# A load ring regrouped from nine 16 KB slots to five 32 KB slots in a decode attention kernel

## The chip, the cores and the metric

The kernel runs on one core of a Trainium2 chip. The metric is device time in microseconds; lower is better. "Span" is the time from the first to the last instruction in a profile or a timed run; the device time was 1.8 to 3.0 us longer in the runs of the record.

## The reference

One decode token attends over a cache of 65,536 keys and values for 4 key-value heads (8 query heads each, head size 128), beside a small gated MLP; a sigmoid gate mixes the two. Cut to what matters:

```python
# x: (1,1,1024); k_cache, v_cache: (1,4,65536,128); wq: (1024,4096); wo: (4096,1024), all bfloat16
g = sigmoid((x * gate_w).sum(-1))
a = softmax(q(x @ wq) @ k.T / sqrt(128)) @ v @ wo      # 8 query heads per k/v head
b = mlp(x, w_in, w_sp, b_sp, w_out)                     # w_in: (1024,3584), w_out: (1792,1024)
out = g * a + (1 - g) * b
```

Every byte of cache and weights is needed once: 162 MB, of which keys and values are 134 MB.

## The kernel before

A recorder notes each operation with what it reads and writes and turns that into semaphore waits. All large loads go from HBM (the chip's main memory) through one ring of buffers, the slots, in SBUF (the core's own memory, 128 partitions) and one queue, issued by SyncE (SP). A *unit* is 16 KB per partition: 8,192 keys of one head, or a piece of weights.

```python
TILES = 64; UK = 128 * TILES          # keys in a unit
NS = 9; SLOT = 8192                   # nine slots of 8192 bf16 = 16 KB per partition
NKTS = 8; NSC = 12                    # buffers for transposed keys, for scores
# [...]
small(vw(xT, 0, [[2, 4], [1, 2]]), A_x[0, 0].rearrange("(i p k) -> p i k", i=4, k=2), "xT")   # 512 pieces of 4 B
small(vw(gw, 0, [[2, 4], [1, 2]]), gate_w.rearrange("(i p k) -> p i k", i=4, k=2), "gw")      # on ScalarE's queue
# [...]
def kv(cache, g, u):
    return cache[0, g, UK * u:UK * (u + 1), :].rearrange("(p x) d -> p (x d)", p=128)
# stream: 4 x wq, keys 0..7 with w_in and w_out between them, then key n and value n-9 in turn, 4 x wo
def issue(upto):
    while issued[0] < min(upto, len(stream)):
        n = issued[0]
        key, src, ln = stream[n]
        s = n % NS
        P("SP", lambda e, n=n, src=src, ln=ln: e.dma_start(slot(n)[:, 0:ln], src), w=[("slot", s)], dma="s%d" % s)
        issued[0] += 1
# [...] the last PE operation that reads a slot is followed by issue(place[key] + NS + 1)
```

A step on TensorE (PE) transposes one key unit (64 transposes), makes its scores, and multiplies the softmax weights of a unit nine steps back with its values. PE's first operation needs the gate vector `gw`; its last is the output projection on the four `wo` loads.

Of the kernel before, what the change touches and what calls it, by code (L numbers as in the profile page):

```python
# [137 lines left out]
def bass_gated_mix__gqa_block_cached__mixer_gmlp__decode_kernel(  # L138
# [25 lines left out]
    TILES = 64  # L164
    UK = 128 * TILES
    NU = Sk // UK
    NS = 9
    SLOT = 8192
    NB = TILES // 8
    NKTS = 8  # L170
    NSC = 12
    QW = DO // 4
    SCALE = 1.0 / math.sqrt(Dh)
    GELU_C = 0.044715
# [52 lines left out]
    def slot(n):  # L227
        return ab("RING", SLOT, (n % NS) * SLOT)

# [28 lines left out]
    def small(dst, src, key):  # L258
        def f(e):
            with nc.allow_non_contiguous_dma(reason="a few bytes"):  # L260
                return e.dma_start(dst, src)
        P("ACT", f, w=[key], dma=key)

    small(vw(xT, 0, [[2, 4], [1, 2]]), A_x[0, 0].rearrange("(i p k) -> p i k", i=4, k=2), "xT")
    small(vw(gw, 0, [[2, 4], [1, 2]]), gate_w.rearrange("(i p k) -> p i k", i=4, k=2), "gw")
    small(wb[:, 0:1], bass.AP(tensor=B_w_sp.tensor, offset=B_w_sp.offset, ap=[[0, 128], [1, 1]]), "wsp")
    small(wb[:, 1:2], bass.AP(tensor=B_b_sp.tensor, offset=B_b_sp.offset, ap=[[0, 128], [1, 1]]), "bsp")


    stream = []  # L270
    place = {}

    def load(key, src, n):
        place[key] = len(stream)
        stream.append((key, src, n))

    def rows(w, i, c):

        return w[128 * c * i:128 * c * (i + 1), :].rearrange("(p c) n -> p (c n)", c=c)

    WQ_N = HQ * Dh

    def kv(cache, g, u):
        return cache[0, g, UK * u:UK * (u + 1), :].rearrange("(p x) d -> p (x d)", p=128)

    KV = [(g, u) for g in range(G) for u in range(NU)]
    for i in range(4):
        load(("wq", i), rows(A_wq, i, 2), 2 * WQ_N)
    steps = []
    for n in range(NU):  # L290
        load(("k", n), kv(A_k_cache, *KV[n]), SLOT)
        aux = None
        if n < 4:
            load(("win", n), rows(B_w_in, n, 2), 2 * F)
            aux = ("win", n)
        elif n in (5, 7):
            i = (n - 5) // 2
            load(("wout", i), rows(B_w_out, i, 7), 7 * DO)
            aux = ("wout", i)
        steps.append((n, None, aux))  # L300
    total = G * NU
    for n in range(NU, total + NU + 1):
        k = n if n < total else None
        v = n - NU - 1
        if k is not None:
            load(("k", k), kv(A_k_cache, *KV[k]), SLOT)
        if v >= 0:
            load(("v", v), kv(A_v_cache, *KV[v]), SLOT)
        else:
            v = None  # L310
        steps.append((k, v, None))
    for i in range(4):
        load(("wo", i), rows(A_wo, i, 8), 8 * DO)

    issued = [0]

    def issue(upto):
        while issued[0] < min(upto, len(stream)):
            n = issued[0]
            assert n < NS or stream[n - NS][0] in used  # L320
            key, src, ln = stream[n]
            s = n % NS
            P("SP", lambda e, n=n, src=src, ln=ln: e.dma_start(slot(n)[:, 0:ln], src), w=[("slot", s)], dma="s%d" % s)
            issued[0] += 1

    used = set()

    def use(key):
        issue(place[key] + 1)
        used.add(key)  # L330
        return slot(place[key]), ("slot", place[key] % NS)

    issue(NS)

# [22 lines left out]
    for i in range(4):  # L357
        sl, key = use(("wq", i))

        def f(e, i=i, sl=sl):  # L360
            for k in range(2):
                for h in range(HQ):
                    ins = e.matmul(pf(OB)[:, h:h + 1], sl[:, WQ_N * k + 128 * h:WQ_N * k + 128 * (h + 1)],  # L363
                                   xT[:, 2 * i + k:2 * i + k + 1], start=(i == 0 and k == 0 and h == 0),
                                   stop=(i == 3 and k == 1), skip_group_check=True)
            return ins
        P("PE", f, r=["xT", key], w=[B(OB)])
        issue(place[("wq", i)] + NS + 1)
    for g in range(G):
        P("DVE", lambda e, g=g: e.tensor_copy(vw(qpad, 128 * g, [[40, 4], [1, 8]]),  # L370
                                              vw(pf(OB), 8 * g, [[0, 4], [1, 8]])),
# [6 lines left out]
    def k_piece(n, j):  # L378
        sl, key = use(("k", n))
        first = nbatch[0]  # L380
        for b in (2 * j, 2 * j + 1):
            i = nbatch[0]
            nbatch[0] += 1
            pb = KTB[i % 4]

            def tr(e, b=b, pb=pb):
                for t in range(8):
                    ins = e.transpose(pbf(pb)[:, 128 * t:128 * (t + 1)],  # L388
                                      sl[:, 128 * (8 * b + t):128 * (8 * b + t + 1)], idb)
                return ins  # L390
            P("PE", tr, r=["idb", key], w=[B(pb)])
            if b in (2, 5, 7):
                P("ACT", lambda e, i=i, pb=pb: e.activation(ktb(i), pbf(pb), ACTF.Copy),  # L393
                  w=[("kt", i % NKTS), B(pb)])
            else:
                P("DVE", lambda e, i=i, pb=pb: e.tensor_copy(ktb(i), pbf(pb)), w=[("kt", i % NKTS), B(pb)])  # L396
        if j == 3:
            issue(place[("k", n)] + NS + 1)
        pend.append((n, j, first))

    def s_piece():
# [46 lines left out]
    def pv_piece(n):  # L448
        g, u = KV[n]
        sl, key = use(("v", n))  # L450

        def f(e):
            for xi in range(4):
                for cg in range(4):
                    ins = e.matmul(pf(OB)[32 * cg:32 * (cg + 1), :],  # L455
                                   ptsb(n)[:, 128 * xi + 32 * cg:128 * xi + 32 * (cg + 1)],
                                   vw(sl, 128 * (4 * cg + xi), [[2048, 4], [1, 128]]),
                                   start=(u == 0 and xi == 0), stop=(u == NU - 1 and xi == 3),
                                   tile_position=(0, 32 * cg), skip_group_check=True)
            return ins  # L460
        P("PE", f, r=[("ptsb", n % 2), key], w=[B(OB)])
        issue(place[("v", n)] + NS + 1)
        if u == NU - 1:
            out_piece(g)

# [30 lines left out]
    def win_piece(i):  # L496
        sl, key = use(("win", i))

        def f(e):
            for k in range(2):  # L500
                for z in range(2 * FC):
                    c0 = F * k + FH * (z // FC) + 128 * 7 * (z % FC // 7) + z % 7
                    ins = e.matmul(pf(MB)[:, z:z + 1], vw(sl, c0, [[7, 128]]), xT[:, 2 * i + k:2 * i + k + 1],  # L503
                                   start=(i == 0 and k == 0 and z == 0), stop=(i == 3 and k == 1),
                                   skip_group_check=True)
            return ins
        P("PE", f, r=["xT", key], w=[B(MB)])
        issue(place[("win", i)] + NS + 1)
        if i == 3:
            mixer_piece()  # L510

# [33 lines left out]
    def wout_piece(i):  # L545
        sl, key = use(("wout", i))

        def f(e):
            for c in range(7):
                for q in range(4):  # L550
                    ins = e.matmul(pf(MB)[32 * q:32 * q + 1, 0:QW], yb[:, 7 * i + c:7 * i + c + 1],  # L551
                                   sl[:, DO * c + QW * q:DO * c + QW * (q + 1)],
                                   start=(i == 0 and c == 0), stop=(i == 1 and c == 6), tile_position=(0, 32 * q),
                                   skip_group_check=True)
            return ins
        P("PE", f, r=["yb", key], w=[B(MB)])
        issue(place[("wout", i)] + NS + 1)
        if i == 1:
            P("ACT", lambda e: e.activation(brow[0:97, :], pf(MB)[0:97, 0:QW], ACTF.Copy), w=["brow", B(MB)])

# [8 lines left out]
    for si, (k, v, aux) in enumerate(steps):  # L569
        nxt = steps[si + 1][1] if si + 1 < len(steps) else None  # L570
        if k is None and pend:
            s_piece()
        if v is not None and v not in started:
            start_exp(v)
        for j in range(4):
            if k is not None:
                k_piece(k, j)
                s_piece() if len(pend) > 1 else None
            if j == 1 and v is not None:
                pt_piece(v)  # L580
            if j == 2 and nxt is not None and (k is not None or not pend):
                start_exp(nxt)
            if j == 3 and v is not None:
                pv_piece(v)
        if v is not None and v % NU == 0:
            weight_piece(v // NU)
        if aux is not None:
            (win_piece if aux[0] == "win" else wout_piece)(aux[1])


    FB = KTB[0]
# [46 lines left out]
```

## Time and profile before

| | before |
|---|---|
| device time, median | 395.0 us (394.81 to 395.49) |
| span in the profile | 393.2 us |
| HBM bytes read | 162.01 MB |
| PE busy | 70% |
| last output weights used from | 388.76 us |

The first view is the page's head, the slices and the DMA part of the kernel before: busy time by engine, then the busy share (tenths) and the GB/s of 40 equal slices of the span, then packets and bytes by queue.

```profile
span 393.2 us, 8544 instructions
...
PE 275.8 (70%) x3902; PEld 195.3 (50%) x3902; DVE 160.4 (41%) x347; ACT 124.3 (32%) x171; POOL 1.5 (0%) x8
...
DMA  8999999999999999999999999999999999999992
GB/s 318 403 427 422 419 429 423 423 423 428 430 427 427 424 425 425 427 427 426 423 423 425 427 428 428 427 428 428 427 425 427 421 428 425 427 426 430 425 397 89
...
q1 hardware_dynamic: 11240, 162.01, 97.3%
q8 instruction: 31, 0.51, 0.5%
q10 hardware_dynamic: 1344, 0.00, 0.2%
...
HBM read 162.01 MB, written 0.00 MB: 412 GB/s over the span
```

The DMA engines hardly rest: 162.01 MB at 427 GB/s are 379 us. PE is not the limit. A packet is one entry of the DMA engines' records; here it holds one row of one partition (9,216 packets of 16 KB for 72 loads of 128 rows). Beside the data queue (q1) stand 31 packets of an instruction queue (q8), 16 KB each, and 1,344 packets (q10) of the small loads.

The chain that ended last, in order of time (start, length, what), shows where compute decides and where loading does. Five of its pieces:

```profile
1.22 38.99 DMA arena<-in_gate_w_dram
...
165.67 35.17 DMA arena<-in_A_k_cache_dram
...
346.71 41.91 DMA arena<-in_A_wo_dram
388.76 1.91 PE pb L598 x26
390.69 0.42 DVE arena L604
```

PE starts after the gate's 39 us, works off its backlog until about 166 us, and from then on waits for loads.

Two readings below come from the records of the trace that the page only sums up: each DMA packet with its start, duration and size, and each increment of a load's semaphore. The profile counts 16 DMA engines, and a load of the kernel before has 16 increments ("landings"). I take one increment as one engine's share of the load, eight of its 128 packets, and their spread as how far apart the engines are. The last load before, with the first landing in us and the offsets of the others in ns:

```
before, last wo load: first landing 381.95
offsets 0 123 135 147 611 776 899 3065 4833 4922 6318 6379 6392 6437 6449 6677
```

Seven engines are within 0.9 us of each other. Eight are 4.8 to 6.7 us behind; one lies between, at 3.1 us. The kernel can end only after the last of them, at 388.62 us. I call the first group the leading engines and the other one the lagging engines. At 47 us this spread is only 0.6 us.

### The profile page before, as it was taken

The numbers are of one execution on the slowest core, as the hardware profiler recorded it, in microseconds if no ns is written. First come the engines' busy times: TensorE is split into PE (matmuls) and PEld (weight loads), VectorE is DVE, ScalarE is ACT, GpSimd is POOL, SyncE is SP. The second block draws the span as 40 slices with busy tenths as digits, with TensorE's granted clock in tenths as the row PEclk, the third lists the DMA queues.
The fourth block names the chain that finished last, engine by engine and source line by source line (L and its number), as shares of the span: only waits on it lengthen the run. The fifth ranks groups of instructions, "written<-read, shape, count | busy, mean of one in ns | idle before, by whom it ended". The sixth has DMA issues, their size and how long they took to land.

```text
span 393.2 us, 8544 instructions
## 1 busy us (share of the span) xinstructions
PE 275.8 (70%) x3902; PEld 195.3 (50%) x3902; DVE 160.4 (41%) x347; ACT 124.3 (32%) x171; POOL 1.5 (0%) x8
## 2 busy tenths in 40 slices
PE   0000699996998999997867686779668875644543
PEld 0000688885776766665645464556445553211121
DVE  2000043446666766576534354466334454200200
ACT  1000033332556555553524242335233334210000
POOL 1000000000000000000000000000000000000000
PEclk9999999886999999998989698889888898555555
DMA  8999999999999999999999999999999999999992
GB/s 318 403 427 422 419 429 423 423 423 428 430 427 427 424 425 425 427 427 426 423 423 425 427 428 428 427 428 428 427 425 427 421 428 425 427 426 430 425 397 89
DMA packets 12620, 162.57 MB, mean 413 GB/s; under 512 B 2596, under 2 KB 2600, under 8 KB 2600
## 3 DMA queue, kind: packets, MB, share of 16 engines
q1 hardware_dynamic: 11240, 162.01, 97.3%
q8 instruction: 31, 0.51, 0.5%
q10 hardware_dynamic: 1344, 0.00, 0.2%
q14 instruction: 5, 0.04, 0.0%
HBM read 162.01 MB, written 0.00 MB: 412 GB/s over the span
## 4 chain that ended last, share of the span: by engine, by line
DMA 60%; PE 31%; DVE 6%; ACT 1%; issue 1%; ACTq 0%; DVEq 0%
DMA arena<-in_A_k_cache_dram 30%; PE pb L388 16%; DMA arena<-in_A_wo_dram 11%; DMA arena<-in_gate_w_dram 10%; DMA arena<-in_A_v_cache_dram 10%; PE pb L410 6%; DVE arena L396 3%; PE pb L503 3%; PE pb L455 2%; PE pb L363 2%; DVE arena L415 2%; PE pb L443 1%; ACT arena L393 0%; PE pb L598 0%; PE pb L551 0%
## 5 line engine op out<-in xcount | busy, mean ns | idle before, releaser
L388 PE MATMUL pb<-arena 128*128 128x128 bf16 x2048 | 154.4, 236 | 27.5 <-DMA arena<-in_A_k_cache_dram 27.5
L388 PEld LDWEIGHTS pb<-arena 128*128 128x128 bf16 x2048 | 133.1, 107 | 55.6 <-DMA arena<-in_A_k_cache_dram 33.1
L396 DVE COPY arena<-pb 128x1024 bf16<-128x1024 bf16 x160 | 108.4, 689 | 109.8 <-PE pb L388 109.0
L393 ACT ACTIVATE arena<-pb 128x1024 bf16<-128x1024 bf16 x96 | 97.9, 1020 | 161.8 <-PE pb L388 161.8
L410 PE MATMUL pb<-arena 128*32 128x512 bf16 x512 | 54.9, 419 | 5.5 <-DVE arena L415 3.6
L455 PE MATMUL pb<-arena 128*32 128x512 bf16 x512 | 40.1, 441 | 19.0 <-DMA arena<-in_A_v_cache_dram 18.3
L455 PEld LDWEIGHTS pb<-arena 128*32 128x32 bf16 x512 | 14.3, 104 | 32.8 <-issue 20.2
L348 PE MATMUL pb<-arena 128*128 128x1 f32 x2 | 0.6, 362 | 40.7 <-DVE arena L347 40.7
L436 ACT ACTIVATE arena<-arena 128x512 bf16<-128x512 f32 x32 | 22.8, 713 | 16.3 <-PE pb L443 14.5
L446 DVE COPY arena<-pb 128x512 bf16<-128x512 bf16 x32 | 13.6, 424 | 30.4 <-PE pb L443 30.4
L410 PEld LDWEIGHTS pb<-arena 128*32 128x32 bf16 x512 | 13.3, 93 | 22.0 <-DVE arena L415 6.6
L415 DVE TENSOR_SCALAR_CACHE_REDUCE arena<-pb 128x512 f32<-128x512 f32 x32 | 21.8, 681 | 2.8 <-PE pb L410 2.8
L348 PEld LDWEIGHTS pb<-arena 128*128 128x128 f32 x2 | 0.5, 310 | 40.7 <-DVE arena L347 40.7
L443 PE MATMUL pb<-arena 128*128 128x128 bf16 x128 | 15.4, 257 | 0.0
L346 DVE TENSOR_TENSOR arena<-arena 128x8 f32<-128x8 bf16 x1 | 0.2, 166 | 37.0 <-DMA arena<-in_gate_w_dram 37.0
L443 PEld LDWEIGHTS pb<-arena 128*128 128x128 bf16 x128 | 9.1, 113 | 11.7 <-issue 11.7
L598 PE MATMUL pb<-arena 128*1 128x256 bf16 x128 | 7.5, 413 | 8.8 <-DMA arena<-in_A_wo_dram 8.8
L503 PEld LDWEIGHTS pb<-arena 128*128 128x128 bf16 x224 | 12.3, 153 | 0.9 <-issue 0.9
L503 PE MATMUL pb<-arena 128*128 128x1 bf16 x224 | 12.6, 192 | 0.0
L350 ACT ACTIVATE arena<-pb 128x1 f32<-128x1 f32 x1 | 0.2, 171 | 34.2 <-PE pb L348 34.2
L598 PEld LDWEIGHTS pb<-arena 128*1 128x1 bf16 x128 | 3.7, 115 | 12.3 <-DMA arena<-in_A_wo_dram 6.7
L363 PE MATMUL pb<-arena 128*128 128x1 bf16 x256 | 7.1, 165 | 1.8 <-issue 1.8
(78 smaller groups left out, 60.5 us busy)
## 6 DMA issues: line engine op xcount, KB each, us to landing
arena<-in_A_k_cache_dram SPq DMA_DIRECT2D x32, 2048.0 KB, 29.9
arena<-in_A_v_cache_dram SPq DMA_DIRECT2D x32, 2048.0 KB, 37.5
arena<-in_A_wq_dram SPq DMA_DIRECT2D x4, 2048.0 KB, 14.8
arena<-in_A_wo_dram SPq DMA_DIRECT2D x4, 2048.0 KB, 41.9
arena<-in_B_w_in_dram SPq DMA_DIRECT2D x4, 1792.0 KB, 22.5
arena<-in_B_w_out_dram SPq DMA_DIRECT2D x2, 1792.0 KB, 15.1
arena<-in_A_x_dram ACTq DMA_DIRECT2D x1, 2.0 KB, 22.3
arena<-in_gate_w_dram ACTq DMA_DIRECT2D x1, 2.0 KB, 39.0
```

The source lines that it names most:

```text
L363: ins = e.matmul(pf(OB)[:, h:h + 1], sl[:, WQ_N * k + 128 * h:WQ_N * k + 128 * (h + 1)], xT[:, 2 * i + k:2 * i + k + 1], start=(i == 0 and ...
L388: ins = e.transpose(pbf(pb)[:, 128 * t:128 * (t + 1)], sl[:, 128 * (8 * b + t):128 * (8 * b + t + 1)], idb)
L393: P("ACT", lambda e, i=i, pb=pb: e.activation(ktb(i), pbf(pb), ACTF.Copy), w=[("kt", i % NKTS), B(pb)])
L396: P("DVE", lambda e, i=i, pb=pb: e.tensor_copy(ktb(i), pbf(pb)), w=[("kt", i % NKTS), B(pb)])
L410: ins = e.matmul(pf(SCB)[32 * cg:32 * (cg + 1), :], qpad[:, 128 * g + 32 * j:128 * g + 32 * (j + 1)], src, start=(j == 0), stop=(j == 3), ...
L415: P("DVE", lambda e: e.tensor_scalar(scs(n), pf(SCB), 0.0, None, op0=ALU.add, op1=ALU.max, accum_out=maxc[:, n:n + 1]), w=[("sc", n % NSC) ...
L436: P("ACT", lambda e: e.activation(psb(n), scs(n), ACTF.Exp, bias=gcol(g, K_NB), scale=SCALE, accum_out=lp[:, n:n + 1]), r=[("sc", n % NSC) ...
L443: ins = e.transpose(pbf(PTB)[:, 128 * xi:128 * (xi + 1)], psb(n)[:, 128 * xi:128 * (xi + 1)], idb)
L446: P("DVE", lambda e: e.tensor_copy(ptsb(n), pbf(PTB)[:, 0:512]), w=[("ptsb", n % 2), B(PTB)])
L455: ins = e.matmul(pf(OB)[32 * cg:32 * (cg + 1), :], ptsb(n)[:, 128 * xi + 32 * cg:128 * xi + 32 * (cg + 1)], vw(sl, 128 * (4 * cg + xi), [[ ...
L503: ins = e.matmul(pf(MB)[:, z:z + 1], vw(sl, c0, [[7, 128]]), xT[:, 2 * i + k:2 * i + k + 1], start=(i == 0 and k == 0 and z == 0), stop=(i ...
L598: ins = e.matmul(pf(FB)[32 * q:32 * q + 1, 0:QW], ovec[:, 8 * i + c:8 * i + c + 1], sl[:, DO * c + QW * q:DO * c + QW * (q + 1)], start=(i ...
```

## The change

Its intent: fewer and larger loads. Two units that are used one after the other come as one load with 32 KB rows; the ring has five slots of 32 KB. To make room, the key-tile and score buffers shrink. A slot is given back only when both of its units are used. The two small vectors follow the new row layout of the weights (four rows per partition together, instead of two), and PE reads the MLP's input weights (`w_in`, the "mixer weights" of the prediction) with a stride of 14 elements instead of 7. The core of the diff, cuts marked:

```diff
-    NS = 9
-    SLOT = 8192
+    NS = 5
+    SLOT = 16384
-    NKTS = 8
-    NSC = 12
+    NKTS = 6
+    NSC = 10
[...]
-    small(vw(gw, 0, [[2, 4], [1, 2]]), gate_w.rearrange("(i p k) -> p i k", i=4, k=2), "gw")
+    small(vw(gw, 0, [[4, 2], [1, 4]]), gate_w.rearrange("(i p k) -> p i k", i=2, k=4), "gw")
[... the same for xT]
-    def kv(cache, g, u):
-        return cache[0, g, UK * u:UK * (u + 1), :].rearrange("(p x) d -> p (x d)", p=128)
+    def kv(cache, n):
+        g, u = KV[n]
+        return cache[0, g, UK * u:UK * (u + 2), :].rearrange("(p x) d -> p (x d)", p=128)
+    def pair(name, cache, n):
+        load([(name, n), (name, n + 1)], [(0, kv(cache, n))])
[... wq, w_in and w_out paired alike; wo stays four single loads]
+    def done(key):
+        n = place[key][0]
+        if key == stream[n][0][-1]:
+            issue(n + NS + 1)
[... done(key) replaces issue(place[key] + NS + 1) at each last use]
```

More of the change, by code (lines that the diff above doesn't have):

```diff
@@ L262, in small @@
         P("ACT", f, w=[key], dma=key)
-    small(vw(xT, 0, [[2, 4], [1, 2]]), A_x[0, 0].rearrange("(i p k) -> p i k", i=4, k=2), "xT")
-    small(vw(gw, 0, [[2, 4], [1, 2]]), gate_w.rearrange("(i p k) -> p i k", i=4, k=2), "gw")
+    small(vw(xT, 0, [[4, 2], [1, 4]]), A_x[0, 0].rearrange("(i p k) -> p i k", i=2, k=4), "xT")
+    small(vw(gw, 0, [[4, 2], [1, 4]]), gate_w.rearrange("(i p k) -> p i k", i=2, k=4), "gw")
     small(wb[:, 0:1], bass.AP(tensor=B_w_sp.tensor, offset=B_w_sp.offset, ap=[[0, 128], [1, 1]]), "wsp")
@@ L271, in bass_gated_mix__gqa_block_cached__mixer_gmlp__decode_kernel, with load @@
     place = {}
-    def load(key, src, n):
-        place[key] = len(stream)
-        stream.append((key, src, n))
+    def load(keys, pieces):
+        for i, key in enumerate(keys):
+            place[key] = (len(stream), i)
+        stream.append((keys, pieces))
     def rows(w, i, c):
@@ L281, in bass_gated_mix__gqa_block_cached__mixer_gmlp__decode_kernel @@
     WQ_N = HQ * Dh
-    def kv(cache, g, u):
-        return cache[0, g, UK * u:UK * (u + 1), :].rearrange("(p x) d -> p (x d)", p=128)
+    def kv(cache, n):
[3 more added lines that the diff above has]
+        load([(name, n), (name, n + 1)], [(0, kv(cache, n))])
     KV = [(g, u) for g in range(G) for u in range(NU)]
-    for i in range(4):
-        load(("wq", i), rows(A_wq, i, 2), 2 * WQ_N)
+    total = G * NU
+    for i in range(0, 4, 2):
+        load([("wq", i), ("wq", i + 1)], [(0, rows(A_wq, i // 2, 4))])
     steps = []
     for n in range(NU):
-        load(("k", n), kv(A_k_cache, *KV[n]), SLOT)
-        aux = None
-        if n < 4:
-            load(("win", n), rows(B_w_in, n, 2), 2 * F)
-            aux = ("win", n)
-        elif n in (5, 7):
-            i = (n - 5) // 2
-            load(("wout", i), rows(B_w_out, i, 7), 7 * DO)
-            aux = ("wout", i)
+        if n % 2 == 0:
+            pair("k", A_k_cache, n)
+        aux = ()
+        if n in (1, 3):
+            load([("win", n - 1), ("win", n)], [(0, rows(B_w_in, n // 2, 4))])
+            aux = (("win", n - 1), ("win", n))
+        elif n == 5:
+            load([("wout", 0), ("wout", 1)], [(0, rows(B_w_out, 0, 14))])
+        elif n == 6:
+            aux = (("wout", 0), ("wout", 1))
         steps.append((n, None, aux))
-    total = G * NU
     for n in range(NU, total + NU + 1):
@@ L304, in bass_gated_mix__gqa_block_cached__mixer_gmlp__decode_kernel @@
         v = n - NU - 1
-        if k is not None:
-            load(("k", k), kv(A_k_cache, *KV[k]), SLOT)
+        if k is not None and k % 2 == 0:
+            pair("k", A_k_cache, k)
         if v >= 0:
-            load(("v", v), kv(A_v_cache, *KV[v]), SLOT)
+            if v % 2 == 0:
+                pair("v", A_v_cache, v)
         else:
             v = None
-        steps.append((k, v, None))
+        steps.append((k, v, ()))
     for i in range(4):
-        load(("wo", i), rows(A_wo, i, 8), 8 * DO)
+        load([("wo", i)], [(0, rows(A_wo, i, 8))])
+    WIDTH = {"wq": 2 * WQ_N, "win": 2 * F, "wout": 7 * DO, "wo": 8 * DO, "k": UK, "v": UK}
     issued = [0]
+    used = set()
     def issue(upto):
@@ L319, in issue, with f @@
             n = issued[0]
-            assert n < NS or stream[n - NS][0] in used
-            key, src, ln = stream[n]
+            assert n < NS or all(k in used for k in stream[n - NS][0])
+            keys, pieces = stream[n]
             s = n % NS
-            P("SP", lambda e, n=n, src=src, ln=ln: e.dma_start(slot(n)[:, 0:ln], src), w=[("slot", s)], dma="s%d" % s)
+            def f(e, n=n, pieces=pieces):
+                for c0, src in pieces:
+                    ins = e.dma_start(slot(n)[:, c0:c0 + src.shape[1]], src)
+                return ins
+            P("SP", f, w=[("slot", s)], dma="s%d" % s)
             issued[0] += 1
-    used = set()
     def use(key):
-        issue(place[key] + 1)
+        n, i = place[key]
+        issue(n + 1)
         used.add(key)
-        return slot(place[key]), ("slot", place[key] % NS)
+        w = WIDTH[key[0]]
+        return slot(n)[:, i * w:(i + 1) * w], ("slot", n % NS)
+    def done(key):
+        n = place[key][0]
+        if key == stream[n][0][-1]:
+            issue(n + NS + 1)
     issue(NS)
@@ L367, in bass_gated_mix__gqa_block_cached__mixer_gmlp__decode_kernel @@
         P("PE", f, r=["xT", key], w=[B(OB)])
-        issue(place[("wq", i)] + NS + 1)
+        done(("wq", i))
     for g in range(G):
@@ L397, in k_piece @@
         if j == 3:
-            issue(place[("k", n)] + NS + 1)
+            done(("k", n))
         pend.append((n, j, first))
@@ L461, in pv_piece @@
         P("PE", f, r=[("ptsb", n % 2), key], w=[B(OB)])
-        issue(place[("v", n)] + NS + 1)
+        done(("v", n))
         if u == NU - 1:
@@ L501, in f @@
                 for z in range(2 * FC):
-                    c0 = F * k + FH * (z // FC) + 128 * 7 * (z % FC // 7) + z % 7
-                    ins = e.matmul(pf(MB)[:, z:z + 1], vw(sl, c0, [[7, 128]]), xT[:, 2 * i + k:2 * i + k + 1],
+                    c0 = F * k + FH * (z // FC) + z % FC
+                    ins = e.matmul(pf(MB)[:, z:z + 1], vw(sl, c0, [[FC, 128]]), xT[:, 2 * i + k:2 * i + k + 1],
                                    start=(i == 0 and k == 0 and z == 0), stop=(i == 3 and k == 1),
@@ L507, in win_piece @@
         P("PE", f, r=["xT", key], w=[B(MB)])
-        issue(place[("win", i)] + NS + 1)
+        done(("win", i))
         if i == 3:
@@ L556, in wout_piece @@
         P("PE", f, r=["yb", key], w=[B(MB)])
-        issue(place[("wout", i)] + NS + 1)
+        done(("wout", i))
         if i == 1:
@@ L586, in bass_gated_mix__gqa_block_cached__mixer_gmlp__decode_kernel @@
             weight_piece(v // NU)
-        if aux is not None:
-            (win_piece if aux[0] == "win" else wout_piece)(aux[1])
+        for a in aux:
+            (win_piece if a[0] == "win" else wout_piece)(a[1])
     FB = KTB[0]
```

## The prediction

An estimate: a *turn* is one small packet of the vectors on an engine, (512 + 512) / 16 pieces and the ends of the two loads, 66 before, and the gate's 39.0 us make 0.59 us of each. The prediction does not say what its 5 ns come from; its two packet times give, by estimate, 611 - 8 x (611 - 535) = 3 ns beyond the bytes of a 16 KB packet. The 0.5 us agree with the page: q10 takes 0.2% of 393.2 us, 0.8 us, and half of that goes. The 1 us of issue latency agrees with the trace: in the kernel before the first load is issued at 0.74 us and its first packet starts at 1.77 us.

> **What bounds the kernel now.** The supply of bytes. In the slice view the 16 DMA engines are at 9 tenths from the second to the 39th of 40 slices, at 420 to 430 GB/s; PE is busy 70%. HBM reads are 162.01 MB: at 427 GB/s that is 379 us of the 393.2 us span. The chain of waits is compute from 41 us (the gate's small load takes 39.0 us) to 166 us; then it is key, value and output-weight loads, with 2.4 us of work behind the last one (388.8 us).
>
> The packet records: a 16 KB packet takes 611 ns, a 14 KB one 535 ns, so time follows bytes. Value loads at the end land 4.89 us apart; 8 packets at a pitch of 608 ns account for 4.86, so 26 ns per load are not bytes. The engines end apart: the DMA share falls from 381 us on, and the landings within one load spread over 6.7 us. That spread grows in jumps of about 1.5 us, with the 31 instruction fetches of 16 KB, which fall on some engines only.
>
> **What the change does.** Same bytes, same matmuls. 74 of the 78 loads become 37 of twice the size, with rows of 32 KB. Removed, by estimate: 37 x 26 ns = 1.0 us of ends of loads; if a row stays one descriptor, half of what one costs beyond its bytes (at most 5 ns x 300 = 1.5 us); half the small descriptors of the two vectors, below 0.5 us. Together 1 to 3 us on every engine, all on the critical path. Untouched: fetches, spread, tail, start.
>
> Added: coarser slots. 20 MB instead of 18 MB lie ahead of PE, but a slot comes free only after both halves. The vectors need 34 turns instead of 66, each behind a packet twice as long, so the gate should again land near 41 us and PE start at 41 to 43. ([...]39.0 us for 66 turns, 0.59 us each, agrees.) With the old PE times the tightest slot is that of keys 4 and 5: free at about 105.3 us, when the queue runs dry at about 108. Less 1 us of issue latency, slack is 1.7 us: a hole of 0 to 2 us is possible. Later slack is 5 us or more (6.7 us of compute per step against 9.8 us of loading). Fewer key-tile and score buffers still leave three pieces and one step: no new wait.
>
> **Predicted time:** 393.3 us, range 390.0 to 397.0. Faster by over 2%: 0.03; within 2%: 0.93; slower: 0.04.
>
> **What would show it.** Right: packets of 32 KB at 1.21 to 1.22 us, a plateau of 428 to 431 GB/s, pairs 9.74 to 9.77 us apart in the value-only stretch, 31 fetches and 6 to 7 us spread again, last output weight at 386 to 388 us, gate near 41 us. Descriptor step wrong: 16 KB packets still, gate near 20 us, gain only 1 us. Ring step wrong: a slice between 105 and 145 us below 410 GB/s, the queue waiting for key transposes.
>
> **What would make it wrong.** 32 KB rows meeting HBM less well (plateau below 420: slower by over 1.5%); a fetch behind a longer packet costing its engine more than 1.5 us, or stalling PE longer; fetches falling on other engines, 1.5 us each way; wider-strided reads of the mixer weights slowing PE before 90 us and opening the hole at 108.

## The result, and the profile after

| | before | after |
|---|---|---|
| device time, median | 395.0 us | 393.2 us (392.14 to 393.55) |
| ratio | 1 | 0.9948 (0.9927 to 0.9969) |
| span in the profile | 393.2 us | 390.4 us |
| loads in the ring | 78 | 41 |
| landing of the last load, leading engine | 381.95 us | 380.48 us |
| same, last engine | 388.62 us | 385.81 us |

Ratios in this document are the mean time of one kernel's fast runs over that of the other's of the same rounds, so they are not quite the ratio of the medians quoted; the brackets are 95% intervals. Where I compare two changed kernels, I divide their ratios to before.

The same parts of the page of the kernel after:

```profile
span 390.4 us, 8502 instructions
...
PE 274.1 (70%) x3902; PEld 194.6 (50%) x3902; DVE 160.2 (41%) x347; ACT 124.4 (32%) x171; POOL 1.5 (0%) x8
...
DMA  8999999999999999999999999999999999999992
GB/s 322 430 430 437 418 412 441 426 428 425 411 405 431 433 426 431 428 431 428 427 431 428 428 431 430 425 435 435 428 431 433 428 426 431 433 431 421 416 415 96
...
q1 hardware_dynamic: 5912, 162.01, 97.1%
q8 instruction: 30, 0.49, 0.5%
q10 hardware_dynamic: 832, 0.00, 0.1%
```

The bytes are the same; the packets of the data queue are nearly halved, so a 32 KB row stayed one packet (its median is 1,214 ns, against 613 ns for 16 KB). In the second half most slices lie at 425 to 435 GB/s, where before they lay at 421 to 430. Two slices, at 98 to 117 us, are low: 411 and 405.

The chain of the kernel after, same columns:

```profile
1.21 39.23 DMA arena<-in_gate_w_dram
...
153.72 24.96 DMA arena<-in_A_k_cache_dram
...
361.59 24.22 DMA arena<-in_A_wo_dram
385.95 1.91 PE pb L621 x32
```

The gate still lands after 39 us, and 1.9 us of PE work still stand behind the last landing, which is 2.8 us earlier.

The low slices have a cause in the issue queue. This is SyncE's own timeline of the kernel after from 85 to 125 us (start, length of the issue, what):

```profile
89.74 0.33 SPq L338 DMA_DIRECT2D arena<-in_A_v_cache_dram  x1
106.72 0.33 SPq L338 DMA_DIRECT2D arena<-in_A_k_cache_dram  x1
114.19 0.33 SPq L338 DMA_DIRECT2D arena<-in_A_v_cache_dram  x1
```

and its waits from 90 to 110 us (us in total, times, longest):

```profile
SPq L338 <- PE pb L411: 16.6, 1, 16.6
```

SyncE waited 16.6 us for the key transposes (line 411) of the pair 4 and 5 and issued the next load at 106.72 us. On the leading engine loads land at 107.08 and then at 118.16 us, 11.08 us apart instead of the usual 9.71. I call these 1.4 us the hole: the queue ran dry (a DMA share of 0.91 at 105 to 110 us), and the first 16 packets after the pause, begun from 107.7 to 108.5 us, were slow as well: 1.25 to 2.32 us against a median of 1.21. It is the hole that the prediction had named.

### The profile page after: what moved, and what is told of

It is laid out like the page before. It is cut to its first block, busy times and chain, and to the rows that moved or that the text cites. A ratio compares the mean times of both kernels' runs of the same rounds, so it can differ in the third digit from the quotient of the medians.

```text
span 390.4 us, 8502 instructions
## 1 busy us (share of the span) xinstructions
PE 274.1 (70%) x3902; PEld 194.6 (50%) x3902; DVE 160.2 (41%) x347; ACT 124.4 (32%) x171; POOL 1.5 (0%) x8
## 4 chain that ended last, share of the span: by engine, by line
DMA 55%; PE 36%; DVE 6%; issue 1%; ACT 1%; ACTq 0%; DVEq 0%
DMA arena<-in_A_k_cache_dram 31%; PE pb L411 18%; DMA arena<-in_gate_w_dram 10%; DMA arena<-in_A_v_cache_dram 8%; PE pb L433 6%; DMA arena<-in_A_wo_dram 6%; PE pb L526 3%; DVE arena L419 3%; PE pb L478 3%; PE pb L386 2%; DVE arena L438 2%; PE pb L466 1%; ACT arena L416 0%; PE pb L621 0%; PE pb L574 0%
## 5 line engine op out<-in xcount | busy, mean ns | idle before, releaser
L526 PE MATMUL pb<-arena 128*128 128x1 bf16 x224 | 13.8, 198 | 0.0
L621 PE MATMUL pb<-arena 128*1 128x256 bf16 x128 | 6.5, 379 | 6.8 <-DMA arena<-in_A_wo_dram 6.8
L386 PE MATMUL pb<-arena 128*128 128x1 bf16 x256 | 7.1, 165 | 2.1 <-issue 2.1
## 6 DMA issues: line engine op xcount, KB each, us to landing
arena<-in_gate_w_dram ACTq DMA_DIRECT2D x1, 2.0 KB, 39.2
```

The source lines that it names most:

```text
L386: ins = e.matmul(pf(OB)[:, h:h + 1], sl[:, WQ_N * k + 128 * h:WQ_N * k + 128 * (h + 1)], xT[:, 2 * i + k:2 * i + k + 1], start=(i == 0 and ...
L526: ins = e.matmul(pf(MB)[:, z:z + 1], vw(sl, c0, [[FC, 128]]), xT[:, 2 * i + k:2 * i + k + 1], start=(i == 0 and k == 0 and z == 0), stop=( ...
L621: ins = e.matmul(pf(FB)[32 * q:32 * q + 1, 0:QW], ovec[:, 8 * i + c:8 * i + c + 1], sl[:, DO * c + QW * q:DO * c + QW * (q + 1)], start=(i ...
```

## Experiments

### Theories

Four questions decide why the time fell by this little and not by more or less.

1. Where does the gain come from: a fixed cost of each packet, or a fixed cost of the end of each load? The prediction had put 1.0 us on ends of loads and at most 1.5 us on packets.
2. Does a hole in the queue cost what it lasts, or do the lagging engines hide it?
3. Are the lagging engines behind because of the instruction fetches, or are some engines slow by themselves?
4. What is behind the last landing worth?

For cleaner experiments I first made `vec16`, the kernel after without the hole, and used it as the base of the others. All runs gave outputs that pass the comparison with the reference.

### vec16: the hole taken away

The two vectors come eight values to a partition, with the weights' rows to match, so PE starts some 17 us earlier.

```diff
-    small(vw(gw, 0, [[4, 2], [1, 4]]), gate_w.rearrange("(i p k) -> p i k", i=2, k=4), "gw")
+    small(gw, gate_w.rearrange("(p k) -> p k", k=8), "gw")
[... the same for xT]
+    def part(w, i):
+        n = w.shape[1]
+        return w.rearrange("(p c) n -> p (c n)", c=8)[:, 4 * n * i:4 * n * (i + 1)]
-        load([("wq", i), ("wq", i + 1)], [(0, rows(A_wq, i // 2, 4))])
+        load([("wq", i), ("wq", i + 1)], [(0, part(A_wq, i // 2))])
[... the same for w_in]
```

Expected:

> The kernel after, with x and the gate vector laid out eight to a partition, so that each takes 9 turns of an engine instead of 17. The gate should land at 20 to 24 us instead of 39, PE start some 18 us earlier, and the hole of the DMA queue near 107 us vanish. Theory 'a hole costs what it lasts': the stream ends 0.5 to 1.9 us earlier than in the kernel after, ratio to before 0.990 to 0.994. Rival 'the lagging engines decide': the hole idled only the engines that were ahead, and let those that carry the instruction fetches catch up; the fast engines then end about 1.5 us earlier, the spread of the last loads' landings goes back from 5.3 to about 6.7 us, and the time stays within 0.5 us of the kernel after: ratio to before 0.994 to 0.996.

Measured: 392.23 us median, ratio 0.9928 (0.9914 to 0.9942), span 390.5 us. The DMA part of its page lists the issue-to-landing time of the gate (KB, then us):

```profile
arena<-in_gate_w_dram ACTq DMA_DIRECT2D x1, 2.0 KB, 21.7
```

The hole is gone: pairs land every 9.71 us from the tenth load on. The leading engine's last landing moved from 380.48 to 379.12 us, by the length of the hole. The last engine's did not move: 385.94 us against 385.81. The spread is 6.82 us instead of 5.34. In these two profiles the hole had cost nothing. By its ratio, though, the run lies in the range of the other theory (0.990 to 0.994); `after_again` below takes that up.

### rows16, rows8 and ends2: packets or ends

`rows16` and `rows8` cut the 32 KB rows of key and value loads into two or four rows, still one load with one end per slot; the keys are assigned to partitions differently, but alike for keys and values.

```diff
-        return cache[0, g, UK * u:UK * (u + 2), :].rearrange("(p x) d -> p (x d)", p=128)
+        return cache[0, g, UK * u:UK * (u + 2), :].rearrange("(h p x) d -> p h (x d)", h=2, p=128)   # rows8: h=4
[...]
-                    ins = e.dma_start(slot(n)[:, c0:c0 + src.shape[1]], src)
+                    ins = e.dma_start(vw(slot(n), c0, [[w, 2], [1, w]]), src)      # w = row; rows8: [w, 4]
```

`ends2` makes of the two halves two DMAs, each with its own 16 increments:

```diff
-                    ins = e.dma_start(vw(slot(n), c0, [[w, 2], [1, w]]), src)
+                    ins = [e.dma_start(slot(n)[:, w * h:w * (h + 1)], src[:, h]) for h in range(2)]
[... both increment the slot's semaphore; users wait for the sum of both]
```

Expected of rows16:

> vec16, with the key and value loads still 4 MB each with one end, but made of 16 KB rows (two per partition). Kernel after: a pair takes 9.708 us on an engine, of which 9.626 is bytes at the rate that fits both kernels, and 0.082 is overhead. Theory 'each packet costs a fixed time' (about 6 ns of it per packet, 34 per end): a pair takes 9.75 to 9.76 us, 32 pairs add 1.5 us, ratio to vec16 1.004. If all overhead is per packet (10 ns): 9.79 us, 2.6 us more, 1.0066. Rival 'only the end of a load costs': 9.71 us as with 32 KB rows, ratio to vec16 1.000.

Expected of rows8:

> As rows16, with 8 KB rows (four per partition), one end per 4 MB. Theory 'each packet costs a fixed time': a pair takes 9.85 us at 6 ns per packet (9.95 at 10 ns), 32 pairs add 4.6 us (7.7 us) to vec16: ratio 1.012 (1.020). Rival 'only the end costs': 9.71 us and no change.

Expected of ends2:

> As rows16, but each key or value pair is two DMAs of 2 MB in the same slot: same 16 KB rows, one end more per pair. Theory 'packets cost, ends little': pair at the value of rows16 plus at most 0.01 us, time within 0.3 us of rows16. Rival 'ends cost 26 to 34 ns each': pair 0.03 us longer than rows16, 32 pairs 1 us, and back at the 9.79 us of the kernel before.

Measured, with the pair time of the leading engine averaged over 16 pairs between about 205 and 365 us (before: 15 pairs of loads; ends2: from the first landing of each pair, 16 pairs from 200 to 357 us):

| kernel | row | ends per pair | us per pair | last engine's last landing | median us | ratio to before |
|---|---|---|---|---|---|---|
| before | 16 KB | 2 | 9.784 | 388.62 | 395.21 | 1 |
| vec16 | 32 KB | 1 | 9.710 | 385.94 | 392.23 | 0.9928 |
| rows16 | 16 KB | 1 | 9.781 | 388.13 | 394.89 | 0.9990 (0.9977 to 1.0004) |
| ends2 | 16 KB | 2 | 9.786 | 388.23 | 394.71 | 0.9982 (0.9971 to 0.9994) |
| rows8 | 8 KB | 1 | 9.928 | 392.90 | 399.62 | 1.0109 (1.0094 to 1.0123) |

Eight packets more per engine and pair (vec16 to rows16) cost 9.781 - 9.710 = 0.071 us, 9 ns per packet. Sixteen more (rows16 to rows8) cost 0.147 us, again 9 ns. A second end per pair (ends2) lengthens a pair by 0.005 us, and moves the last landing by 0.10 us over 32 pairs (0.23 us on the leading engine): 3 to 7 ns each. Two profiles of one kernel, vec16 and vec16_again, differ by 0.08 us in their last landing, so the size is rough; but it is not the 26 to 34 ns of the rival. The median time is not longer either. The slices of rows8 show the lower plateau, to be held against the 425 to 435 of the kernel after:

```profile
GB/s 340 452 334 447 402 439 409 433 411 419 420 421 421 420 421 421 420 420 420 420 419 420 420 421 422 420 420 420 420 420 421 420 418 421 421 420 424 430 397 91
```

So "each packet costs a fixed time" stands and "only the end costs" falls. The size is 9 ns, between the two values that had been written down for it. (A packet more is also a row more here; which of the two costs is not separated.) By estimate, without that part a pair takes 9.71 - 8 x 0.009 = 9.64 us for 262,144 bytes per engine, 27.2 GB/s, or 435 GB/s for sixteen. Most slices in the second half of the kernel after lie at 425 to 435 GB/s.

The change removed 624 - 328 = 296 packets per engine (8 per load, 78 and 41 loads): at 9 ns this is 2.7 us. The last engine's last landing moved by 388.62 - 385.94 = 2.7 us in vec16. The experiment shows 2.2 us of this (rows16 to vec16, 388.13 - 385.94: the rows of keys and values alone); the other 0.5 us, from the rows of the weights, the ends and the vectors, is not separated.

### hole_short and hole_long: holes made on purpose

One load (keys 24 and 25) is held back until a chosen key unit has been transposed; nothing else changes.

```diff
+    HOLD, REL = 25, ("k", 22)            # hole_long: ("k", 23)
[...]
+            if n == HOLD and not free[0]:
+                return
-            P("SP", f, w=[("slot", s)], dma="s%d" % s)
+            P("SP", f, r=["rel"] if n == HOLD else [], w=[("slot", s)], dma="s%d" % s)
[... the last transposes of REL write "rel" and set free]
```

Expected of hole_short:

> vec16, with the load of keys 24 and 25 held back on purpose until the transposes of key unit 22 are done (about 245.3 us). The engines that are ahead run dry at about 243.0 us and get new packets at about 246.4: a hole of some 3.4 us for them. The engines that carry the instruction fetches are 5.2 us behind and still have packets until about 248. Theory 'a hole costs what it lasts': 3.4 us more than vec16, ratio to vec16 1.009. Theory 'the lagging engines decide': their lag falls from 5.2 to about 1.8 us, the spread of the last load's landings from 6.8 to about 3.4 us, and the time stays within 0.5 us of vec16, ratio 1.000.

Expected of hole_long:

> The same hold, until key unit 23's transposes are done (about 252 us, first packets at 253.1): a hole of about 10 us for the leading engines and 4.9 us for the lagging ones. Theory 'a hole costs what it lasts': 10 us more than vec16, ratio 1.026. Theory 'the lagging engines decide': only the part beyond the lag counts, 4.5 to 5.5 us more, ratio 1.012 to 1.014, with a spread of 1.5 to 2.5 us at the end.

The windows of hole_short, from 235 to 260 us (window, length, busy time of PE, PEld, DVE, ACT and POOL with counts, PE clock, DMA share, GB/s):

```profile
235.00:240.00 5.00, 1.44 (x14) 1.44 (x15) 0.36 (x1) 0.00 (x0) 0.00 (x0) 0.68 1.02 439
240.00:245.00 5.00, 5.00 (x54) 3.40 (x52) 3.43 (x7) 1.27 (x2) 0.00 (x0) 0.64 0.78 334
245.00:250.00 5.00, 4.79 (x80) 3.31 (x76) 2.86 (x7) 3.23 (x5) 0.00 (x0) 1.00 0.74 259
250.00:255.00 5.00, 3.93 (x64) 2.56 (x60) 2.14 (x4) 2.83 (x5) 0.00 (x0) 1.00 0.99 426
```

The same of hole_long:

```profile
240.00:245.00 5.00, 5.00 (x52) 3.49 (x49) 3.22 (x7) 1.15 (x2) 0.00 (x0) 0.60 0.76 328
245.00:250.00 5.00, 4.79 (x80) 3.33 (x76) 2.86 (x7) 3.23 (x5) 0.00 (x0) 1.00 0.12 49
250.00:255.00 5.00, 4.04 (x64) 2.56 (x60) 2.25 (x4) 2.94 (x5) 0.00 (x0) 1.00 0.39 102
```

For comparison, vec16 in the first two of these stretches:

```profile
240.00:245.00 5.00, 5.00 (x66) 3.71 (x65) 3.48 (x8) 2.01 (x3) 0.00 (x0) 0.81 1.05 452
245.00:250.00 5.00, 4.79 (x78) 3.20 (x76) 3.28 (x7) 2.67 (x5) 0.00 (x0) 1.00 1.02 436
```

In hole_short the share falls to about three quarters, not to zero: the lagging engines still work. In hole_long it falls to 0.12. From the landings around the held load:

| | hole of the leading engine | hole of the last engine | last landing against vec16 (385.94) | ratio to before | ratio to vec16 |
|---|---|---|---|---|---|
| hole_short | 257.75 - 242.92 - 9.71 = 5.1 us | 1.4 us | +1.4 us | 0.9961 | 1.0033 (1.3 us) |
| hole_long | 264.64 - 243.09 - 9.71 = 11.8 us | 7.9 us | +7.7 us | 1.0117 | 1.0190 (7.5 us) |

(The ratios to vec16 divide ratios from two chips. Against `vec16_again`, on the chip of these two runs, the holes cost 1.0 and 7.1 us.) Both holes were 1.7 to 1.8 us longer than I had estimated, so the written sizes are missed: the loads were issued 0.8 us later than I had read off vec16 (246.08 and 252.88 us), and the first packets after the pause were slow. In hole_long they began 1.0 us after the issue, about as expected, but the first of each engine took 1.7 to 2.2 us instead of 1.21. The relation is settled all the same: the time lost is the hole of the last engine, not that of the leading one. A hole of 5.1 us on the leaders cost 1.3 us. It is not simply what exceeds the lag: in hole_short the last engine was 5.3 us behind and should have lost nothing by that rule, but the first packet after the pause was slow on all 16 engines (1.4 to 2.3 us).

### half_transposes: fewer instruction fetches

Every second key transpose is left out, so the kernel computes something else. (Its output still passed the comparison with the reference, which shows that this comparison does not catch such an error.) The loads are the same.

```diff
-                for t in range(8):
+                for t in range(0, 8, 2):
[... the four PSUM banks are zeroed once at the start]
```

Expected:

> vec16 with every second key transpose left out (wrong results on purpose; same loads): 2048 fewer PE instructions, hence about 8 of the 31 instruction fetches fewer. Theory 'the fetches, dealt in turn to 8 of the 16 engines, make the lag, 1.5 us each': at most 3 instead of 4 per engine, final spread 5.2 to 5.4 us instead of 6.8, time 1.2 to 1.6 us less than vec16, ratio 0.996 to 0.997. Rival 'some engines are slower by themselves (memory, bus)': spread 6.8 us as before and the same time within 0.3 us.

Measured: 391.1 us median, ratio 0.9894 (0.9881 to 0.9908), against vec16 0.9966 (1.3 us less), against vec16_again of the same chip 0.9958 (1.7 us less). The instruction queue in its page's DMA part:

```profile
q8 instruction: 22, 0.36, 0.4%
```

Eight fetches fewer than the 30 of the kernel after, for 2,048 PE instructions fewer: 256 instructions per fetch. The final spread is 5.19 us instead of 6.82, and the last landing 384.46 us instead of 385.94, while the leading engine stays (379.27 against 379.12). The fetches make the lag, about 1.5 us each. In vec16 the largest lag grows at about 33, 107, 194 to 204 and 292 us, and the 1st, 9th, 17th and 25th fetches begin at 30.3, 102.2, 197.2 and 291.0 us: which fits a deal in turn to the same eight engines. The lags of single landings say so too, though the records of packets do not name their engine. In vec16 eight engines are 1.6 to 2.0 us behind at 97 us, after 8 fetches, and eight are 3.1 to 3.6 us behind at 185 us, after 16. At the end six are 6.3 to 6.8 us behind and two 4.7 us; in half_transposes it is six at 4.4 to 5.2 us and two at 3.5 us. That is 30 = 6 x 4 + 2 x 3 and 22 = 6 x 3 + 2 x 2 fetches. (One more engine lags by 3.3 us in both, for a reason not looked into.) The cost of a fetch is not hidden here: eight fewer end the stream 1.5 us earlier. The packet of a fetch takes a median of 1.08 us by itself (before; 1.06 us after), against 0.61 us for a data packet of the same size; where the rest of the 1.5 us goes stays open.

### tail: less work behind the last landing

```diff
-    for i in range(4):
-        load([("wo", i)], [(0, rows(A_wo, i, 8))])
+    WO = [(0, 0, 8), (1, 0, 8), (2, 0, 8), (3, 0, 6), (3, 6, 8)]
+    for i, c0, c1 in WO:
+        load([("wo", i, c0)], [(0, rows(A_wo, i, 8)[:, DO * c0:DO * c1])])
[... the matmuls follow the same list]
```

Expected:

> vec16 with the last output-weight load of 2 MB cut into 1.5 MB and 0.5 MB, so that only 8 of its 32 matmuls stand behind the last landing: 0.5 us of PE work instead of 1.9. If the end is 'last landing plus what is behind it', 1.2 to 1.5 us less than vec16, ratio 0.996 to 0.997, the best kernel so far at about 391 us. If the small load lands later for its own fixed cost of some 10 ns per packet, nothing of this is lost; a gain below 0.5 us would mean that something else ends the kernel.

Measured: 391.59 us median, ratio 0.9909 (0.9894 to 0.9924), span 389.2 us. It is the fastest correct kernel here: 1.3 us of span less than vec16, but only 0.9981 of its time by ratio (0.75 us); against vec16_again on the same chip it is 0.9973 (1.1 us). The end of its timeline:

```profile
384.78 1.87 PE L626 MATMUL pb<-arena 128*1 128x256 bf16 x32 [1.89 <-DMA arena<-in_A_wo_dram]
385.92 0.23 PEld L626 LDWEIGHTS pb<-arena 128*1 128x1 bf16 x8 [0.20 <-DMA arena<-in_A_wo_dram]
386.71 0.42 DVE L632 TENSOR_TENSOR arena<-pb,arena 97x256 bf16<-97x256 f32 x1 [12.28 <-PE pb L626]
```

The last 8 weight loads start at 385.92 us, at the last landing, and VectorE follows 0.8 us later; before, PE alone took 1.9 us there.

### after_again and vec16_again: the hole's price on one chip

Expected of after_again:

> The kernel after, unchanged, on one chip with the two runs below. If a hole shorter than the lag costs nothing, its time is that of vec16 within 0.5 us (ratio 0.9925 to 0.9945 to before), though its leading engines end 1.4 us later; if the hole costs what it lasts, it is 1.4 us slower than vec16 (0.9965). Its earlier runs scattered between two spans, 390.2 to 390.4 and 391.4 to 391.6; the scatter of about one instruction fetch's worth (1.2 to 1.5 us) is expected to show again, and vec16 not to have it.

Expected of vec16_again:

> As the first time: spans of 390.2 to 390.5 us, ratio to before 0.992 to 0.994, spread of the last landing 6.6 to 6.9 us, keeping to one span where after_again scatters.

Measured on one chip: after_again 393.63 us, ratio 0.9965 (0.9952 to 0.9979); vec16_again 392.38 us, 0.9936 (0.9924 to 0.9949). The spans of the five runs were 390.7, 390.9, 391.8, 391.4 and 391.0 for after_again, 390.4 to 390.6 for vec16_again. So the mean cost of the hole is not nothing: 0.7 us by the mean spans (391.2 against 390.5) and 1.1 us by the ratios, between the two theories as I had written them. The profile of after_again (span 390.7) does not show it: a hole of 1.6 us, a final spread of 5.29, the last landing at 386.12 us against 386.02 in vec16_again.

### after_third: one profile more of the kernel after

Expected:

> The kernel after once more, for its profile alone, since its unprofiled spans scatter from 390.2 to 391.8 us. Theory 'the hole is absorbed, and the scatter is how much of it': if this profile has a span above 391.2 us, its hole near 107 us is longer than the 1.4 us of the other two profiles, or the engines that got a fetch next to it kept more of their lag (final spread above 5.4 us). If the span is near 390.5 again with a hole of 1.4 us and a spread of 5.3 us, the scatter stays open.

Measured: one run, 394.05 us, span 391.7, from the slower end of the scatter. Its hole is the shortest of the three profiles, and it cost the most:

| profile of the kernel after | hole on the leading engine | spread two loads later (127 to 128 us) | final spread | last landing |
|---|---|---|---|---|
| first | 1.4 us | 2.2 us | 5.34 us | 385.81 us |
| after_again | 1.6 us | 2.1 us | 5.29 us | 386.12 us |
| after_third | 0.8 us | 4.1 us | 7.11 us | 387.16 us |

In the first two the engine that ends last had caught up during the hole. In the third it had not, and by 127 us one engine was 4.1 us behind. In this profile the hole was paid in full: the leading engine ends 0.9 us later than in vec16, the last engine 1.2 us later. A fetch began at 105.7 us here, just before the hole, and at 103.2 and 103.3 us in the others. That the place of this fetch decides it is likely but argued only: the records of packets do not name their engine.

### lead8: moving bytes to the leading engines, which failed

If half of the engines are behind by 6.8 us, giving them fewer of the last bytes should gain up to 3 us. The 1.5 MB load of `tail` is made of 16 DMAs of 8 partitions. I assumed that each of these would use the same eight engines; no run had shown that. The clause with it is cut from the expectation, and its "those 8" are these.

```diff
+                if by8:      # the load ("wo", 3, 0)
+                    src = pieces[0][1]
+                    return [e.dma_start(slot(n)[p:p + 8, 0:src.shape[1]], src[p:p + 8]) for p in range(0, 128, 8)]
```

Expected:

> The kernel tail, with its 1.5 MB load of output weights made of 16 DMAs of 8 partitions each[...]. If the lagging engines decide the end and the 8 leading ones are those 8, the laggards have 3.65 us less to do and the leaders 3.65 us more: the spread before the last load shrinks to 1 to 3 us and the kernel ends 2.5 to 3.3 us earlier than tail, spans near 386.3 us. If the laggards are those 8, it ends 3 to 4 us later than tail, spans near 393 us, with a spread near 14 us before the last load. If the two groups are mixed, it ends 3 to 4 us later as well with all spreads grown. No change at all would mean that all 16 engines took part.

Measured: 401.6 us, ratio 1.0169 (1.0154 to 1.0184), spans 398.5 to 399.6: worse than each forecast. The windows of its end, same columns as above:

```profile
375.00:380.00 5.00, 2.45 (x44) 0.98 (x36) 0.00 (x0) 0.00 (x0) 0.00 (x0) 0.50 0.91 219
380.00:385.00 5.00, 0.00 (x0) 0.00 (x0) 0.00 (x0) 0.00 (x0) 0.00 (x0) 0.50 0.83 188
385.00:390.00 5.00, 1.88 (x32) 0.93 (x32) 0.00 (x0) 0.00 (x0) 0.00 (x0) 0.50 0.58 147
```

The engines are busy (a share of 0.91 and 0.83 from 375 to 385 us) and move half the bytes (219 and 188 GB/s): a 12 KB packet has a median of 818 ns here, against 461 ns in tail. The cause was not shown: no run here separates one reason from another.

The trace answers part of what this run was to find out. The load's semaphore shows 16 increments while the DMAs are issued, one per DMA, and 128 as data lands, eight per DMA, which I read as eight engines for each. Of the seven engines that led on the load before, two went straight on to the load after it, whose first landings came at 376.91 and 377.21 us and the third only at 385.41. If all 16 DMAs used the same eight engines, five of the eight were leaders and three were not: the two groups are mixed, and this cut could not have balanced them. Which engines the leading ones are stays open.

## Why the prediction was right

The time, 393.3 us, met the measured 393.2 us, inside the range and inside "within 2%". Point by point:

- **What bounds the kernel.** Right. DMA stayed at 9 tenths in all slices but the first and the last, and the end is the last landing plus 2.4 us (385.95 to 388.33 us).
- **What is gained: right in sum, wrong in its terms.** "1 to 3 us on every engine" is the measured 2.7 us of packets. But the terms were mis-sized both ways. "37 x 26 ns = 1.0 us of ends of loads" measured 3 to 7 ns per end in ends2, 0.1 to 0.3 us. "At most 5 ns x 300 = 1.5 us" of descriptors measured 9 ns x 296 = 2.7 us. The error lay in reading the 608 ns pitch of single packets and the 4.89 us pitch of loads as if their difference had to belong to the end of a load. The rates by row length settle it. That the sum came out right is partly luck: one term was too large by about what the other was too small, and the hole then took back 0.7 to 1.1 us. Where the prediction looked for pairs 9.74 to 9.77 us apart, they came every 9.71. The part of the vectors is seen only in the start: the first 4 MB landed at 12.7 instead of 13.0 us on the leading engine.
- **The marks of the mechanism.** Packets of 32 KB took 1,214 ns (1.21 to 1.22 us predicted), the gate took 39.2 us to land from its issue (landing near 41 us predicted, 40.4 found). The first shows one packet per row. The second fits turns that each wait for about one data packet: 39.0 us / 66 = 0.59 us before (packets of 0.61 us), 39.2 / 34 = 1.15 us after (1.21 us), 21.7 / 18 = 1.21 us in vec16.
- **The hole.** Right in place, cause and size: 106.7 us, waiting for the transposes of keys 4 and 5, 0.8 to 1.6 us in three profiles. The slice at 107 to 117 us fell to 405 GB/s, which was the mark I had set for the ring step being wrong; the prediction had allowed a hole of 0 to 2 us in the same step, and that is what it was. What the prediction did not see is that such a hole is not simply lost time. Deliberate holes of 5.1 and 11.8 us cost 1.3 and 7.5 us, since only what reaches the lagging engines counts. In the kernel after it cost 0.7 to 1.1 us on average.
- **The spread of the engines, "untouched".** Its cause, the instruction fetches, was right, and half_transposes shows it. The spread itself was not untouched: 5.3 us in two profiles and 7.1 us in one, through the hole.
- **Fewer tile and score buffers, wider weight strides.** The buffers made no new wait that the page shows; the busy times of PE, VectorE and ScalarE differ by at most 1%. The mixer's input weights, which the prediction had named as a risk to the hole, did slow PE a little: PE's timelines give 3.15 us for the 56 matmuls of a unit before and 6.88 us for the 112 of two units after (below, one stretch of each), 1.2 us more over four units. The slot of keys 4 and 5 came free at 106.7 us instead of the 105.3 forecast. The granted clock was lower after (0.63 and 0.67 in the two stretches, 1.00 before), but that is not the cause: within the first stretch it falls from 1.00 to 0.50 at 64.7 us, and these matmuls start every 60 ns on both sides of the fall, against 53 ns before. What else differs in them is the stride.

```profile
57.44 3.15 PE L503 MATMUL pb<-arena 128*128 128x1 bf16 x56
62.81 6.88 PE L526 MATMUL pb<-arena 128*128 128x1 bf16 x112
```

The sum, for the first profile: 388.62 - 2.7 (packets) = 385.9 us, found 385.81. In the timed runs the median gain is 1.8 us, and the hole's scatter (spans of 390.2 to 391.8 us) accounts for the rest.

## What to carry to other kernels

On the one saturated load queue of this kernel, larger loads gained the number of packets saved per DMA engine times the fixed cost of one: 296 x 9 ns = 2.7 us, 0.7% of the time. Find that cost for yours by changing the row length alone, and don't book it on the number of loads (a further end of a load cost 3 to 7 ns here). Look at the landings of each load by engine: this kernel ended with the engines that also carry the instruction fetches, 5.3 to 7.1 us behind the leading ones, so a hole of 5.1 us in the queue cost 1.3 us, and 2,048 instructions fewer on PE, which is busy 70% of the kernel after, were worth 1.3 to 1.7 us. And check what a coarser ring does to the first slot that comes back: here an earlier start of PE (the two vectors in fewer pieces) took the hole of 0.8 to 1.6 us away.
